# Newton's steps of a second batch on the whole array, and an uneven last tile, in a planned attention and FFN kernel

## The chip, the cores and the metric

The kernel runs on one core of a Trainium2 chip. Times are device microseconds of one execution. Before the change the median of three runs is 261.45 us (261.41 to 261.6). The profile is of one further execution, which took 260.83 us.

The core's engines are PE (matrix products, with its weight loads shown as PEld), DVE and ACT (elementwise work), POOL (which here issues most loads, and does a little elementwise work) and SP (which issues the stores). Each runs its own instructions in order and waits on semaphores for the others.

## The reference

For each of 8 batches and 8 heads, with 576 tokens of 64 dimensions, attention is approximated through 32 landmarks, each the mean of 18 consecutive tokens. Three small softmax matrices are formed; the middle one is inverted by six Newton steps. The result goes through a feed-forward layer with a squared relu (4608 tokens, 512 to 2048 to 512).

```python
A = sm(q, k_lm)
Bm = sm(q_lm, k_lm)
C = sm(q_lm, k)
Z = Bm.transpose(0, 1, 3, 2) / (norm1(Bm) * norminf(Bm) + 1e-06)
for _ in range(6):
    Z = 2 * Z - Z @ Bm @ Z
x = A @ Z @ C @ v
h = x @ w_in
g = np.maximum(h, 0.0) ** 2
return g @ w_out
```

## The kernel before

All work is cut into named steps. A step is declared by `op(name, engines, emit, R, W, ...)`: the engines that may do it with an assumed duration for each, what it reads and writes, and the PSUM banks it needs. `Plan.schedule` (line 134) then runs a list schedule at build time: among the ready steps of an engine the one with the largest `tail` goes first, and where two engines may do a step, the one that ends it first by the plan gets it. `tail` is the length of the work that follows a step, plus an entry for the kind and batch in the table `URGE` (line 1302); `LEAN` (line 1318) shifts the choice between ACT and DVE. The result fixes which engine does each step and in what order. On the chip nothing is reordered: an engine that comes to a step whose input isn't there waits, and everything behind it waits too.

The steps of a batch b that the text names:

- `ld…`, `win`, `wout`, `la`: loads, issued by POOL in the planned order. They are spread over eight semaphores, so a load is issued only when the eighth before it has landed. X holds q and k, V holds v, AC landmark sums that DMA forms for batches 4 to 7.
- `T` (line 576, DVE): transposes of q and k, four a batch. `lm` (lines 593 and 600, PE) sums tokens to landmarks; `lmc`, `lme`, `lmt` bring them to SBUF (ACT, DVE).
- `SC`, `SA`, or `SS` where both are merged (lines 720 and 709, PE): the products for C and A. `B` (line 691): that for Bm.
- `Bmx`, `Bsb`, `Bex`, `Bsu`, `Brc`, `Bml`, `Btf`, `Btr`, `Bcs`, `Bct`, `Bnm`, `Bad`, `Brn`, `Zi`, `Yi` (lines 765 to 852, mostly DVE, `Bex` and sometimes `Btr` on ACT): softmax of Bm, its norms, and Newton's starting values. `BBT` is Bm times its transpose.
- `N` and `U` (lines 874 or 879, and 888): one Newton step is a product on PE and an update on DVE. For batches in `TILED` the eight heads are eight separate 32x32 products per step (line 879). For the others (`whole`) the heads are put on the diagonals of two 128x128 matrices BD by `bd` (line 827; `bt` does so for `BBT`), on POOL or DVE, and two whole-array products do the step (line 874).
- `Cmx`, `Cng`, `Cex`, `Crc`, `Cnr`, `CT`: softmax of C and its transpose. `CV` (line 939): C times v. `Zm`, `ZC` (line 978): Newton's result times that; `ZCe` copies it. `W` (line 1002) multiplies it with w_in, `We` copies the result to WP (a copy of 128x1024).
- `At`, `Amx`, `Asb`, `Aex`, `Asu`, `Arc`, `Aml`, `Ab` (lines 1043 to 1063; `Aex` on ACT, the rest on DVE): softmax of A in two parts, transposed to AT.
- `F` (line 1105, PE): blocks of the first FFN product, from WP and AT. Batches 0 and 1 have 32 blocks (16 of 320 columns, then 16 of 256), the others 16 of 576. `R` (line 1123 on ACT, 1125 on DVE) is the relu, `Q` (line 1132 on ACT, 1134 on DVE) the square into G. PSUM for F is limited to four banks, and RS, between R and Q, has three buffers.
- `O` (line 1152, PE): the second FFN product, 36 tiles of 128 tokens, each in four steps of four 512-column products. `Oe` copies a tile out of PSUM, `St` stores it. The last tile, 35, is done in two parts of 256 columns (steps O35.0 to O35.7), each with its own copy and stores, so that the last store is small. The stores of the first part are both issued by SP, those of the second by SP and ACT.

Until the first O step, fill products (line 1258) keep PE busy in its gaps; they compute nothing that is used.

Of the kernel before, what the change touches and what calls it, by code (L numbers as in the profile page):

```python
# [8 lines left out]
P = 128  # L9
AF = mybir.ActivationFunctionType  # L10
ALU = mybir.AluOpType
AX = mybir.AxisListType
# [8 lines left out]
M = 32  # L21
SEG = S // M
HALF = S // 2
D_MODEL = 512
# [3 lines left out]
N_TILE = N_TOK // P  # L28
# [3 lines left out]
A_LEN = (10, 8)  # L32
# [304 lines left out]
def v_(n, fast=False):  # L337
    return 0.07 + (0.00052 if fast else 0.00104) * n
# [21 lines left out]
def pos_a(c, r):  # L360
    return (c + r + 2) % 4
# [18 lines left out]
def kernel(  # L380
# [106 lines left out]
    def eng(e):  # L487
        return {"ACT": nc.scalar, "DVE": nc.vector, "POOL": nc.gpsimd}[e]
# [46 lines left out]
    def attention(b):  # L535
# [197 lines left out]
        def sCA(e, i):  # L733
            u = i ^ int(pSs[0].at > pSs[1].at)
            for w in range(2):
                for r in range(2):
                    for c in range(4):
                        mmC(c, r, w, u, pSs[i].at + r)
                        mmA(c, r, w, i)
# [8 lines left out]
        if merged:  # L748

            for i in range(2):  # L750
                with_b = i == 0 and b in B_SS
                op(f"SS{b}.{i}", {"PE": 0.42 if with_b else 0.32},
                   lambda e, i=i, with_b=with_b: [sCA(e, i), with_b and sB(e, pSs[0], HALF)],
                   R=[*kA(0), *kA(1)], W=[pSs[i], pAs[i]], alloc=[pSs[i], pAs[i]], mode="32x32",
                   ni=96 if with_b else 64)
        late = [x for t in range(2) for r in range(2) for x in kts(t, r)] if b in B_LATE else []
        if b in B_SS:
            pB, oB = pSs[0], HALF
        else:
            op(f"B{b}", {"PE": 0.14}, lambda e: sB(e, pB, 0), R=[kLT(0), kLT(1), *late], W=[pB],  # L760
               alloc=[pB], mode="64x32" if by_pe else "32x32", ni=16 if by_pe else 32)
# [148 lines left out]
        for r in range(2):  # L910
            R = [*pSs] if merged else [pSs[r]]
            op(f"Cng{b}.{r}", {"DVE": 0.07}, lambda e, r=r: nc.vector.tensor_scalar(  # L912
                out=s_[:, 12 + r:13 + r], in0=s_[:, 12 + r:13 + r], scalar1=-SCALE / SEG,
                scalar2=None, op0=ALU.mult), R=[kb(f"cmx{r}")], W=[kb(f"cmx{r}")])
            op(f"Cex{b}.{r}", {"ACT": a_(576) + 0.27}, lambda e, r=r: nc.scalar.activation(  # L915
                Cs[r][:].rearrange("p x u -> p u x"), cbanks(r),
                AF.Exp, bias=s_[:, 12 + r:13 + r], scale=SCALE / SEG,
                accum_out=s_[:, 14 + r:15 + r]),
               R=[*R, kb(f"cmx{r}")], W=[("C", r), kb(f"csm{r}")], after=[*o_mx[1:], *([o_bsb] if b in B_SS else [])] if merged else ())
            op(f"Crc{b}.{r}", {"DVE": 0.1}, lambda e, r=r: nc.vector.reciprocal(  # L920
                s_[:, 14 + r:15 + r], s_[:, 14 + r:15 + r]), R=[kb(f"csm{r}")], W=[kb(f"csm{r}")])
            op(f"Cnr{b}.{r}", {"DVE": 0.29, "ACT": 0.66}, lambda e, r=r: copy(
                e, Cs[r][:].rearrange("p x u -> p (x u)"), Cs[r][:].rearrange("p x u -> p (x u)"),
                scale=s_[:, 14 + r:15 + r]), R=[("C", r), kb(f"csm{r}")], W=[("C", r)], port=("DVE",))
            op(f"CT{b}.{r}", {"DVE": 0.02 + v_(288)}, lambda e, r=r: nc.vector.transpose(
                CT[:, :, r].rearrange("p s m e -> p s (m e)").bitcast(U32),
                Cs[r][:].rearrange("p (s m) u -> p s (m u)", s=9).bitcast(U32)),
               R=[("C", r)], W=[("CT", r)])
# [87 lines left out]
        def sA(e, us):  # L1016
            for u in us:
                for w in range(2):
                    for c in range(4):
                        for r in range(2):  # L1020
                            mmA(c, r, w, u)
        for us in () if merged else ((0,), (1,)) if b in SPLIT_A else ((0, 1),):

            op(f"SA{b}.{us[0]}",
               {"PE": sum(pe(M * A_LEN[u], 1 if by_pe else 2) for u in us) + 0.02},
               lambda e, us=us: sA(e, us), after=[o_bcs, o_bbt] if b in SA_LATE else (),
               R=kA(0), W=[pAs[u] for u in us], alloc=[pAs[u] for u in us],
               mode="64x32" if by_pe else "32x32", ni=(16 if by_pe else 32) * len(us))
        for u in range(2):
# [3 lines left out]
            ksa = ("SA", u)  # L1033
            fl = lambda a: a[:].rearrange("p r s m -> p (r s) m")
            pairs = lambda a: a[:].rearrange("p r (s e) m -> p (r s) e m", e=2)
            bA = lambda i, sx=sx, n=n: sx[:, i].rearrange("p r s -> p (r s)").unsqueeze(2) \
                .to_broadcast([P, 2 * n, M])
            bE = lambda i, sx=sx, n=n: sx[:, i].rearrange("p r (s e) -> p (r s) e", e=2) \
                .unsqueeze(3).to_broadcast([P, n, 2, M])

            def aT(e, sa=sa, pS=pS, n=n):
                for z in range(2):
                    nc.vector.transpose(sa[:, z].rearrange("p s m -> p (s m)"),  # L1043
                                        ps[:, pS.at + z, 0:M * n])
            op(f"At{b}.{u}", {"DVE": 2 * v_(M * n)}, aT, R=[pS], W=[ksa])
            op(f"Amx{b}.{u}", {"DVE": v_(nn)}, lambda e, sa=sa, sx=sx: nc.vector.tensor_reduce(
                sx[:, 0].rearrange("p r s -> p (r s)"), fl(sa), axis=AX.X, op=ALU.max),
               R=[ksa], W=[("amx", u)])
            op(f"Asb{b}.{u}", {"DVE": v_(nn), **({"POOL": g_(nn)} if b in POOL_A else {})},
               lambda e, sa=sa, bA=bA: eng(e).tensor_tensor(fl(sa), fl(sa), bA(0), ALU.subtract),  # L1050
               R=[ksa, ("amx", u)], W=[ksa], port=("POOL", "DVE"))
            op(f"Aex{b}.{u}", {"ACT": a_(nn)}, lambda e, sa=sa: nc.scalar.activation(  # L1052
                fl(sa), fl(sa), AF.Exp, scale=SCALE / SEG), R=[ksa], W=[ksa])
            op(f"Asu{b}.{u}", {"DVE": v_(nn)}, lambda e, sa=sa, sx=sx: nc.vector.tensor_reduce(
# [85 lines left out]
    def ffn2(ti):  # L1140
# [1 line left out]
        i = ti % N_OS  # L1142
        f2_ops[ti] = []

        parts = ((0, 256), (256, 512)) if ti == N_TILE - 1 else ((0, D_MODEL),)
        for h, (c0, c1) in enumerate(parts):
            po = Bank(1, "o")
            w = c1 - c0
# [11 lines left out]
            def st(e, js, c0=c0, c1=c1):  # L1160
                for j in js:
                    b, s = divmod(2 * ti + j, 9)
                    rows = out[b * S:(b + 1) * S, c0:c1].rearrange(
                        "(m s e) c -> s m e c", s=9, e=2)[s]
                    (nc.scalar if e == "ACT" else nc.sync).dma_start(
                        rows, OS[i][64 * j:64 * j + 64, c0:c1])
# [1 line left out]
               lambda e, c0=c0, c1=c1, po=po: copy(e, OS[i][:, c0:c1], bank(po)[:, 0:c1 - c0]),  # L1168
               R=[po], W=[("OS", i, h)] + ([("OS", i, 1)] if len(parts) == 1 else []))
            R = [("OS", i, h)] + ([("OS", i, 1)] if len(parts) == 1 else [])  # L1170
            if h == 0:
                op(f"St{ti}", {"SP": 1.2}, lambda e, st=st: st(e, (0, 1)), R=R, W=[],
                   nbytes=512 * w, queue="hw")
            else:
                op(f"St{ti}.1", {"SP": 0.6}, lambda e, st=st: st(e, (0,)), R=R, W=[],
                   nbytes=256 * w, queue="hw")
                op(f"St{ti}.2", {"ACT": 0.6}, lambda e, st=st: st(e, (1,)), R=R, W=[],
                   nbytes=256 * w, queue="hw")


# [81 lines left out]
    with tc.manual_schedule():  # L1262
        for o in sorted(pl.ops, key=lambda o: (o.start, o.seq)):
# [3 lines left out]
PLAN_OUT = None  # L1267
FIRST_LOADS = [("kq", 0), ("v", 0), ("k", 1), ("q", 1), ("win", 0), ("win", 1), ("v", 1), ("wout", 0),
               ("wout", 1), ("wout", 2), ("wout", 3)]
TILED = (0, 1)  # L1270
CRIT = {"lm", "lmc", "lme", "lmt", "lte", "B", "Bmx", "Bsb", "Bex", "Bsu", "Brc", "Bml", "Bmb", "Btf", "Bct", "Btr", "Bcs",
        "Bnm", "Bad", "Brn", "BBT", "Zi", "Yi", "N", "U", "ZC", "ZCe", "W", "We", "AZ", "Az"}
CRIT_B = (0,)
# [7 lines left out]
LM_RANK = (4,)  # L1281

AZ = ()

B_SS = ()

# [13 lines left out]
STRETCH = (1.2, 2.5)  # L1300

URGE = {
# [13 lines left out]
}  # L1316

LEAN = {
# [4 lines left out]
}  # L1323
POOL_A = ()
POOL_M = ()
# [40 lines left out]
```

## Time and profile before

| what | value |
| --- | --- |
| median of three runs | 261.45 us |
| profiled execution | 260.83 us, span 259.1 us |
| granted TensorE clock | 1.00 |
| PE busy | 241.3 us (93%) |
| DVE busy | 209.3 us (81%) |
| ACT busy | 177.7 us (69%) |
| POOL busy | 77.6 us (30%) |
| second FFN product (line 1152) on PE | 133.2 us busy in 553 recorded products |
| first FFN product (line 1105) on PE | 76.9 us busy in 512 products |
| fill products (line 1258) | 10.7 us busy |
| loads by POOL (software queue) | 29.89 MB, 63.9% of 16 engines' span |

A busy PE in such a table is not a PE at its peak, since products overlap and their ends are modelled. What a step costs PE is read from the start of its first weight load to that of the next step. So taken, four 512-column products of line 1152 take 0.86 us, and eight 288-column ones of line 1105 0.98 us.

### The profile page before, as it was taken

What the parts mean: (1) busy time and instruction counts of PE and PEld (TensorE: products, weight loads), DVE (VectorE), ACT (ScalarE), POOL (GpSimd) and SP (SyncE); (2) the same over time, 40 slices, a digit from 0 to 9 for tenths busy, and PEclk for the clock granted to TensorE, in tenths of its full rate; (3) what the DMA queues carried; (4) which work ended last, traced back from release to release, by engine and by line L of the source; (5) the groups of instructions that cost most, each with busy time, mean ns of one, the idle gap of its engine ahead of it and who ended that gap; (6) DMA issues with size and microseconds to landing.
All of it is one profiled execution on the core that took longest, in us unless ns stands there. A gap on an engine that the chain in (4) does not pass through costs nothing.

```text
span 259.1 us, 7447 instructions
## 1 busy us (share of the span) xinstructions
PE 241.3 (93%) x2945; PEld 133.3 (51%) x2987; DVE 209.3 (81%) x614; ACT 177.7 (69%) x362; POOL 77.6 (30%) x111
## 2 busy tenths in 40 slices
PE   5779899998998999999999999999999999999993
PEld 1535355445545456565553456466445654466552
DVE  2599999998979999999999999966896689564200
ACT  2123899586989688885746799899586775597410
POOL 8444532346463437343346054210010000000000
PEclk9999999999999999999999999999999999999999
DMA  5999999999999999999989999482104102111043
GB/s 99 203 195 206 207 206 210 228 253 263 224 208 240 228 284 225 198 180 260 188 138 151 303 154 188 77 152 50 44 22 102 44 23 62 43 40 43 20 102 81
DMA packets 25730, 39.80 MB, mean 154 GB/s; under 512 B 4832, under 2 KB 13408, under 8 KB 25696
## 3 DMA queue, kind: packets, MB, share of 16 engines
q0 software_dynamic: 19776, 29.89, 63.9%
q1 hardware_dynamic: 5840, 9.38, 13.2%
q8 instruction: 23, 0.38, 0.5%
q14 instruction: 11, 0.09, 0.1%
q10 hardware_dynamic: 80, 0.07, 0.1%
HBM read 46.14 MB, written 9.44 MB: 214 GB/s over the span
## 4 chain that ended last, share of the span: by engine, by line
PE 59%; DMA 23%; DVE 9%; ACT 4%; issue 3%; POOL 1%; SPq 0%; ACTq 0%; POOLq 0%
PE ps L1152 35%; PE ps L1105 17%; DMA X<-in_q_dram 10%; DMA V<-in_v_dram 7%; DMA w_in<-in_moe_w_in_dram 4%; PE ps L1002 2%; DMA out_dram<-OS 2%; ACT RS L1123 2%; PE ps L939 1%; PE ps L720 1%; DVE G L1134 1%; POOL X L506 1%; DVE TT L576 1%; ACT OS L493 1%; PE ps L874 1%
## 5 line engine op out<-in xcount | busy, mean ns | idle before, releaser
L1152 PE MATMUL ps<-w_out,G 128*128 128x512 bf16 (+1 forms) x553 | 133.2, 373 | 4.0 <-issue 1.9
L1123 ACT ACTIVATE RS<-ps 128x576 bf16<-128x576 f32 (+2 forms) x153 | 77.5, 560 | 12.6 <-PE ps L1105 10.3
L1152 PEld LDWEIGHTS <-G 128*128 128x128 bf16 x592 | 53.7, 98 | 53.4 <-issue 6.5
L1105 PE MATMUL ps<-AT,WP 128*128 128x288 bf16 (+2 forms) x512 | 76.9, 286 | 1.8 <-ACT RS L1123 0.6
L1105 PEld LDWEIGHTS <-WP 128*128 128x128 bf16 x512 | 48.0, 97 | 26.9 <-issue 4.3
L1134 DVE TENSOR_TENSOR G<-RS 128x576 bf16<-128x576 bf16 (+2 forms) x111 | 44.0, 406 | 7.6 <-ACT RS L1123 6.4
L493 ACT COPY OS<-ps 128x512 f32<-128x512 f32 (+1 forms) x34 | 19.6, 578 | 25.9 <-PE ps L1152 22.8
L576 DVE STREAM_TRANSPOSE TT<-X 128x576 uint32<-128x576 uint32 x32 | 24.0, 764 | 6.7 <-DMA X<-in_k_dram 5.2
L493 ACT CAST WP<-ps 128x1024 bf16<-128x1024 f32 x24 | 23.4, 1018 | 4.0 <-PE ps L1002 3.9
L1132 ACT ACTIVATE G<-RS 128x256 bf16<-128x256 bf16 (+2 forms) x49 | 24.1, 523 | 0.6
L888 DVE SCALAR_TENSOR_TENSOR ST<-ST,ps 128x128 bf16<-128x128 bf16 (+1 forms) x48 | 12.8, 266 | 9.7 <-PE ps L874 8.9
L634 POOL DMA_DIRECT2D AC<-in_k_dram x12 | 12.7, 1056 | 21.2 <-DMA AC<-in_k_dram 14.2
L1052 ACT ACTIVATE SA<-SA 128x640 f32<-128x640 f32 (+1 forms) x16 | 11.0, 687 | 9.6 <-DVE SA L1050 9.5
L515 POOL DMA_DIRECT2D V<-in_v_dram x24 | 13.3, 602 | 13.7 <-DMA w_out<-in_moe_w_out_dram 5.8
L639 POOL DMA_DIRECT2D AC<-AC x8 | 10.4, 1301 | 21.4 <-DMA AC<-in_q_dram 12.0
L634 POOL DMA_DIRECT2D AC<-in_q_dram x12 | 14.5, 1208 | 5.1 <-DMA AC<-in_q_dram 3.9
L915 ACT ACTIVATE C<-ps,sm 128x576 bf16<-128x576 f32 x16 | 13.9, 900 | 2.3 <-DVE sm L912 2.2
L1043 DVE STREAM_TRANSPOSE SA<-ps 128x320 f32<-128x320 f32 (+1 forms) x32 | 13.4, 456 | 0.8 <-PE ps L709 0.8
L506 POOL DMA_DIRECT2D X<-in_k_dram x16 | 9.2, 575 | 13.7 <-DVE TT L576 2.9
L497 DVE CAST WP<-ps 128x1024 bf16<-128x1024 f32 x8 | 9.7, 1210 | 3.7 <-PE ps L1002 3.0
L1060 DVE TENSOR_TENSOR An<-SA,smA 128x640 bf16<-128x640 f32 (+1 forms) x16 | 12.5, 790 | 0.1
L1258 PE MATMUL ps<-onesb 128*128 128x512 bf16 x32 | 10.7, 459 | 2.0 <-DVE onesb L462 1.5
(93 smaller groups left out, 263.6 us busy)
## 6 DMA issues: line engine op xcount, KB each, us to landing
out_dram<-OS SPq DMA_DIRECT2D x70, 128.0 KB, 3.9
X<-in_k_dram POOLq DMA_DIRECT2D x16, 288.0 KB, 10.3
X<-in_q_dram POOLq DMA_DIRECT2D x16, 288.0 KB, 10.7
AC<-in_k_dram POOLq DMA_DIRECT2D x12, 384.0 KB, 9.0
AC<-in_q_dram POOLq DMA_DIRECT2D x12, 384.0 KB, 10.3
V<-in_v_dram POOLq DMA_DIRECT2D x8, 288.0 KB, 10.3
w_in<-in_moe_w_in_dram POOLq DMA_DIRECT2D x8, 256.0 KB, 10.4
w_out<-in_moe_w_out_dram POOLq DMA_DIRECT2D x4, 512.0 KB, 12.0
```

The lines of the kernel that those rows point to most:

```text
L493: nc.scalar.copy(o, i)
L515: lambda e, r=r, p0=p0, n=n, src=src: nc.gpsimd.dma_start(vv[32 * p0:32 * (p0 + n), r].rearrange("p s d -> p (s d)"), src),
L576: op(f"T{b}.{t}{r}", {"DVE": v_(576)}, lambda e, r=r: nc.vector.transpose(tt[:, t, r].rearrange("p s m e -> p (s m e)").bitcast(U32), x[:, ...
L634: lambda e, h=h, t=t, src=src: nc.gpsimd.dma_start(flat(ac[:, 2 * t:2 * t + 2]), src[:, :, 6 * D * h:6 * D * h + 6 * D], **(dict(accum_op= ...
L888: nc.vector.scalar_tensor_tensor(out=o, in0=i0, scalar=2.0, in1=bank(pN)[:, 0:2 * w].rearrange("p (r w) -> p r w", r=2), op0=ALU.mult, op1 ...
L915: op(f"Cex{b}.{r}", {"ACT": a_(576) + 0.27}, lambda e, r=r: nc.scalar.activation(Cs[r][:].rearrange("p x u -> p u x"), cbanks(r), AF.Exp, ...
L1043: nc.vector.transpose(sa[:, z].rearrange("p s m -> p (s m)"), ps[:, pS.at + z, 0:M * n])
L1105: nc.tensor.matmul(ps[:, ph.at + i, 0:w], lhsT=wp[:, r, 128 * f:128 * f + 128], rhs=at[:, r, w * i:w * i + w], start=(r == 0), stop=(r == 1))
L1123: nc.scalar.activation(o, x, AF.Relu)
L1132: nc.scalar.activation(o, x, AF.Square)
L1134: nc.vector.tensor_tensor(o, x, x, ALU.mult)
L1152: nc.tensor.matmul(bank(po)[:, 0:c1 - c0], lhsT=G[:, f, lo:lo + P], rhs=w_out[:, f, c0:c1], start=(f == 0), stop=(f == NF - 1))
```

## The change

Three things change. `TILED` goes from (0, 1) to (0,), so batch 1's Newton steps use block diagonals on the whole array as those of batches 2 to 7 do. The last tile is cut at column 384 instead of 256, and the stores of both of its parts are issued by SP and ACT. And `URGE` and `LEAN` are replaced by other tables, so that the plan comes out with another order and another sharing between the engines.

```diff
@@ ffn2
-        parts = ((0, 256), (256, 512)) if ti == N_TILE - 1 else ((0, D_MODEL),)
+        parts = ((0, LAST_CUT), (LAST_CUT, 512)) if ti == N_TILE - 1 else ((0, D_MODEL),)
...
-            if h == 0:
+            if len(parts) == 1:
                 op(f"St{ti}", {"SP": 1.2}, lambda e, st=st: st(e, (0, 1)), R=R, W=[],
                    nbytes=512 * w, queue="hw")
             else:
-                op(f"St{ti}.1", {"SP": 0.6}, lambda e, st=st: st(e, (0,)), R=R, W=[],
+                op(f"St{ti}.{2 * h}", {"SP": 0.6}, lambda e, st=st: st(e, (0,)), R=R, W=[],
                    nbytes=256 * w, queue="hw")
-                op(f"St{ti}.2", {"ACT": 0.6}, lambda e, st=st: st(e, (1,)), R=R, W=[],
+                op(f"St{ti}.{2 * h + 1}", {"ACT": 0.6}, lambda e, st=st: st(e, (1,)), R=R, W=[],
                    nbytes=256 * w, queue="hw")
@@ tables
-TILED = (0, 1)
+TILED = (0,)
...
+A_ROWS = ()
+A_STEP = 2
+
+LAST_CUT = 384
...
 URGE = {
-    "Ab1": -3.3, "Ab5": 32.5, "Aex2": -0.5, "Aex3": 2.2, "Aml3": -10.4, "Aml4": 2.6, "Aml5": 2.2,
...
+    "Ab0": -1.2, "Ab1": 8.8, "Aex2": -27.4, "Aex4": -5.4, "Aml0": 50.9, "Amx7": 5.5,
...
 LEAN = {
-    "CVe4": -1.87, "CVe7": 0.33, "Cnr1": 0.06, "Cnr6": 0.37, "Oe0": 0.09, "Oe1": -0.12,
...
+    "CVe3": 0.2, "CVe6": -0.23, "Cnr1": 0.11, "Cnr2": -3.21, "Cnr5": -6.27, "Oe1": 0.07,
...
```

The diff also adds a second way to form A's products (`sAr`, used for batches in `A_ROWS`) and moves an offset used only for batches in `B_SS`. Both tuples are empty, so no instruction comes from them. `Amx` and `Asb` address their operands through four dimensions instead of two merged ones; the instructions keep their shapes.

Pieces of the orders that come out, old above new, PE first:

```
lm0.0 lm0.1 SC0.0 B0 SC0.1 BBT0 Bcs0 SA0.0 SA0.1 N0.0 N0.1 N0.2 lm1.0 N0.3 CV0 N0.4 N0.5 B1 ZC0 W0.0 W0.1 F0.0
lm0.0 SC0.0 lm0.1 SC0.1 B0 BBT0 Bcs0 SA0.0 SA0.1 N0.0 N0.1 lm1.0 N0.2 CV0 N0.3 N0.4 N0.5 ZC0 W0.0 W0.1 B1 F0.0

O3.0 O3.1 O3.2 lm3.0 SS2.0 O3.3 F1.0 B2 F1.1 F1.2 F1.3 F1.4 F1.5 F1.6 B3 F1.7 F1.8 O4.0 F1.9 F1.10 O5.0 BBT2 O4.1 F1.11 N2.0 F1.12 F1.13
O3.1 B2 O3.2 lm3.0 SS2.0 F1.0 O3.3 F1.1 F1.2 F1.3 F1.4 F1.5 F1.6 F1.7 BBT2 F1.8 B3 F1.9 F1.10 F1.11 F1.12 N2.0 O5.0 F1.13
```

Around F1's start, ACT and then DVE, in the same way:

```
Oe3.0 R1.0 R1.1 R1.2 Q1.0 Q1.1 Bex2 R1.3 R1.4 R1.5 R1.6 Aex2.0 R1.7 R1.8 Bex3 Q1.6 Q1.7 R1.9
R1.0 Q1.0 Btr2 Oe3.0 R1.1 R1.2 R1.3 Q1.1 Q1.2 Q1.3 R1.4 R1.5 Q1.4 R1.6 R1.7 R1.8 Bex3 Q1.7 R1.9

T3.01 At2.0 lme3.0 Amx2.0 Bmx2 Asb2.0 Bsb2 lmt3.0 Q1.2 Bsu2 Bmx3 Brc2 Q1.3 Bml2 Bsb3 Btf2
T3.01 Bmx2 Ab1.0 Bsb2 Asu1.1 Bsu2 Arc1.1 Brc2 Aml1.1 Bml2 Ab1.1 Btf2
```

Block-diagonal products (`bd`, `bt`) by engine: before, 4 on POOL and 38 on DVE; after, 14 on POOL and 35 on DVE. Among those on POOL are now two of batch 1 and all six `bd` of batch 2.

More of the change, by code (lines that the diff above doesn't have):

```diff
@@ L752, in attention @@
                 op(f"SS{b}.{i}", {"PE": 0.42 if with_b else 0.32},
-                   lambda e, i=i, with_b=with_b: [sCA(e, i), with_b and sB(e, pSs[0], HALF)],
+                   lambda e, i=i, with_b=with_b: [sCA(e, i), with_b and sB(e, pAs[0], M * A_LEN[0])],
                    R=[*kA(0), *kA(1)], W=[pSs[i], pAs[i]], alloc=[pSs[i], pAs[i]], mode="32x32",
@@ L757, in attention @@
         if b in B_SS:
-            pB, oB = pSs[0], HALF
+            pB, oB = pAs[0], M * A_LEN[0]
         else:
@@ L918, in attention @@
                 accum_out=s_[:, 14 + r:15 + r]),
-               R=[*R, kb(f"cmx{r}")], W=[("C", r), kb(f"csm{r}")], after=[*o_mx[1:], *([o_bsb] if b in B_SS else [])] if merged else ())
+               R=[*R, kb(f"cmx{r}")], W=[("C", r), kb(f"csm{r}")], after=o_mx[1:] if merged else ())
             op(f"Crc{b}.{r}", {"DVE": 0.1}, lambda e, r=r: nc.vector.reciprocal(
@@ L1021, in sA, with sAr @@
                             mmA(c, r, w, u)
-        for us in () if merged else ((0,), (1,)) if b in SPLIT_A else ((0, 1),):
+        rows = b in A_ROWS
+        def sAr(e, u, s0, s1):
+            for s in range(s0, s1):
+                for w in range(2):
+                    for c in range(4):
+                        for r in range(2):
+                            nc.tensor.matmul(
+                                ps[quad(pos_a(c, r)), pAs[u].at + r, M * s:M * s + M],
+                                lhsT=tt[quad(c), 0, r, A_LEN[0] * u + s, :, w],
+                                rhs=lt[quad(c), 1, r, :, w], start=(w == 0), stop=(w == 1))
+        for u in range(2) if rows else ():
+            for s0 in range(0, A_LEN[u], A_STEP):
+                op(f"SA{b}.{u}{s0 // A_STEP}", {"PE": 0.22 * A_STEP + 0.02},
+                   lambda e, u=u, s0=s0: sAr(e, u, s0, s0 + A_STEP),
+                   after=[o_bcs, o_bbt] if b in SA_LATE else (), R=kA(0), W=[pAs[u]],
+                   alloc=[] if s0 else [pAs[u]], mode="32x32", ni=32 * A_STEP)
+        for us in () if merged or rows else ((0,), (1,)) if b in SPLIT_A else ((0, 1),):
             op(f"SA{b}.{us[0]}",
@@ L1035, in attention @@
             pairs = lambda a: a[:].rearrange("p r (s e) m -> p (r s) e m", e=2)
-            bA = lambda i, sx=sx, n=n: sx[:, i].rearrange("p r s -> p (r s)").unsqueeze(2) \
-                .to_broadcast([P, 2 * n, M])
             bE = lambda i, sx=sx, n=n: sx[:, i].rearrange("p r (s e) -> p (r s) e", e=2) \
@@ L1044, in aT @@
                                         ps[:, pS.at + z, 0:M * n])
[L1045 to L1048, printed above, removed]
+            if rows:
+                raw = lambda pS=pS, n=n: pair(pS, M * n).rearrange("p r (s m) -> p r s m", m=M)
+                kraw = pS
+            else:
+                raw, kraw = lambda sa=sa: sa[:], ksa
+                op(f"At{b}.{u}", {"DVE": 2 * v_(M * n)}, aT, R=[pS], W=[ksa])
+            op(f"Amx{b}.{u}", {"DVE": v_(nn)}, lambda e, raw=raw, sx=sx: nc.vector.tensor_reduce(
+                sx[:, 0], raw(), axis=AX.X, op=ALU.max), R=[kraw], W=[("amx", u)])
             op(f"Asb{b}.{u}", {"DVE": v_(nn), **({"POOL": g_(nn)} if b in POOL_A else {})},
-               lambda e, sa=sa, bA=bA: eng(e).tensor_tensor(fl(sa), fl(sa), bA(0), ALU.subtract),
-               R=[ksa, ("amx", u)], W=[ksa], port=("POOL", "DVE"))
+               lambda e, sa=sa, sx=sx, raw=raw, n=n: eng(e).tensor_tensor(
+                   sa[:], raw(), sx[:, 0].unsqueeze(3).to_broadcast([P, 2, n, M]), ALU.subtract),
+               R=[kraw, ("amx", u)], W=[ksa], port=("POOL", "DVE"))
             op(f"Aex{b}.{u}", {"ACT": a_(nn)}, lambda e, sa=sa: nc.scalar.activation(
```

33 rows, old and new, of tables (LEAN, URGE) are left out of this document.

## The prediction

> **What bounds the kernel now.** I read the page first (busy shares, the slices, the chain that ended last), then busy time by stretch, then the chain and the timelines of single engines. Steps are named as in the code: N1.3 is Newton's product 3 of batch 1, U its update, F1.5 the sixth block of the first FFN matrix for batch 1, R and Q its relu and square, O7.2 a quarter of output tile 7, lm the landmark sums. Each engine runs in order, so rows can be counted off against the written order of both programs.
>
> ```profile
> PE 241.3 (93%) x2945; PEld 133.3 (51%) x2987; DVE 209.3 (81%) x614; ACT 177.7 (69%) x362; POOL 77.6 (30%) x111
> ...
> PE   5779899998998999999999999999999999999993
> ...
> DVE  2599999998979999999999999966896689564200
> ...
> PE 59%; DMA 23%; DVE 9%; ACT 4%; issue 3%; POOL 1%; SPq 0%; ACTq 0%; POOLq 0%
> ```
>
> PE is busy nearly throughout, and DVE is as full until slice 26 (about 168 us). The chain is DMA first, then PE.
>
> ```profile
> 52.00:61.00 9.00, 7.94 (x140) 4.33 (x136) 7.67 (x16) 6.22 (x10) 4.32 (x7) 1.00 1.09 265
> 61.00:69.00 8.00, 7.59 (x78) 4.27 (x77) 7.90 (x35) 7.49 (x22) 4.95 (x8) 1.00 1.11 239
> 69.00:85.00 16.00, 14.84 (x153) 7.93 (x153) 13.96 (x52) 13.91 (x41) 6.94 (x10) 1.00 1.13 221
> ...
> 121.00:142.00 21.00, 20.78 (x224) 10.74 (x227) 20.85 (x62) 11.56 (x23) 9.52 (x11) 1.00 0.91 176
> ```
>
> Columns: length, busy PE, PEld, DVE, ACT, POOL, granted clock, DMA share, GB/s. PE idles 1.06 us in 52 to 61 and 1.16 us in 69 to 85, but only 0.22 us in 121 to 142: behind 110 us there is almost nothing left to gain.
>
> ```profile
> 47.75 11.00 DMA X<-in_q_dram
> 58.75 0.14 issue
> 58.89 1.18 PE ps L600 x36
> ```
>
> This is the last place where a load sets the pace: lm3.0 waits for the q of batch 3. O3.2, the step ahead, starts at 57.04, so 1.81 us pass where four 512-column products take 0.86: a wait of 0.95 us.
>
> **The sum.** The profiled execution took 260.83 us (span 259.1, 1.73 around it), 0.62 below the median of 261.45. I add differences to the profiled time and move the result up by 0.62. The diff names two edits, but it also replaces the tables that set the order of all steps, so the order is where the time can go.
>
> (a) Newton of batch 1. Per product eight 32-row matmuls become two (56 pairs of weight load and matmul against 14), and 7 block-diagonal products are added: five on DVE at 0.20 (rows of L827, start to next start), two on POOL at 0.69. On PE, N steps of either kind take 0.15 to 0.17 us: nothing. The DVE's 1.0 us lies in a stage where DVE is full, but its work from Bmx0 to Bmx2, added up row by row, is 44.4 us in the new order and 46.8 in the old, because other steps move to ACT and POOL. In itself the edit costs 0, with the outcome in (b).
>
> (b) The start, up to lm3.0.
>
> ```profile
> 18.55 0.24 PE L879 MATMUL ps<-ST 32*32 32x64 bf16 x8 [0.22 <-DVE ST L888]
> 19.18 0.24 PE L879 MATMUL ps<-ST 32*32 32x64 bf16 x8 [0.40 <-DVE ST L888]
> 19.35 2.14 PE L593 MATMUL ps<-X,ident 128*128 128x256 bf16 x18
> 21.42 0.24 PE L879 MATMUL ps<-ST 32*32 32x64 bf16 x8
> ...
> 28.07 0.72 PE L1105 MATMUL ps<-AT,WP 128*128 128x320 bf16 x4 [0.38 <-ACT WP L493]
> ```
>
> The 2.1 us of lm1.0 stand ahead of N0.3 now, and ahead of N0.2 in the new order; they can't start sooner, since they wait for a load. So four Newton steps instead of three follow them, at 0.63 each (18.55 to 19.18). Aml0.0 and Arc0.0 (0.96 us of DVE) now stand between U0.5 and the last Zm, and Amx0.1 and Asb0.1 (1.2 us) among the updates; as the updates leave DVE part of that time anyway, I add 0.3: F0.0 comes about 0.9 us late. What of it reaches lm3.0? PE's wait of 0.95 there would swallow it whole (0). Against that, U1.5 has 41.7 us of DVE rows ahead of it instead of 38.6, which moves ZC1 and W1 from 51.2 to about 55, close to lm3.0; then all 0.9 arrives. I take +0.6, ends 0 and +0.9.
>
> (c) F1.0 to F1.13.
>
> ```profile
> 61.99 1.10 ACT L1123 ACTIVATE RS<-ps 128x320 bf16<-128x320 f32 x3
> 62.97 0.83 ACT L1132 ACTIVATE G<-RS 128x320 bf16<-128x320 bf16 x2
> 63.69 0.26 ACT L769 ACTIVATE Bl<-Bl 128x64 f32<-128x64 f32 x1
> 63.84 1.42 ACT L1123 ACTIVATE RS<-ps 128x320 bf16<-128x320 f32 x4
> ```
>
> A relu costs ACT 0.35 us, a square there 0.38, and F may run four blocks ahead of R. Before, O4.0, O4.1 and O5.0 stand among F1.0 to F1.12: PE has 13 x 0.27 + 3 x 0.86 + 0.5 for the small steps = 6.6 us and takes 7.54 (61.09 to 68.63), 0.9 lost. In the new order F1.1 to F1.12 have no O between them; O3.3 and O5.0 stand at the two ends. ACT's row up to R1.9 holds ten relus, six squares, Btr2 (0.24), Oe3.0 (0.55) and Bex3 (0.26): 3.5 + 2.3 + 1.05 = 6.8 us. PE has 3.5 + 1.7 + 0.4 = 5.6. Also, Btr2 stands second in ACT's row and needs Btf2, which is queued on DVE behind the last transpose of batch 3 and 2.9 us of other rows: up to 1 us more. All relus of F1 are queued behind it, and F1.5 waits for them. So 1.2 to 2.3 us are lost in place of 0.9: +0.3 to +1.4. I take +1.1, near the upper end, because the transpose that Btf2 stands behind waits for the same load as lm3.0.
>
> (d) F1.13 to about 110 us. Before, 41.2 us pass from F1.13 (68.63) to F3.0 (109.83) for 38.6 us of PE work, counted with F at 0.21 and 0.49, O at 0.86, N and BBT at 0.15, SS at 0.45, CV at 0.76, ZC at 0.27, W at 0.29: 2.6 us lost. The O4 tile, kept back, can fill such holes; six block-diagonal products of batch 2 (1.2 us) and two evictions of WP (1.13 each) leave DVE. Ends: 0 and -2.6; between 69 and 85 PE's idle time proper is 1.16, and of that I take most, -0.9.
>
> (e) The last tile.
>
> ```profile
> 253.26 0.37 ACT L493 COPY OS<-ps 128x256 f32<-128x256 f32 x1 [1.16 <-PE ps L1152]
> 255.07 0.42 DVE L497 COPY OS<-ps 128x256 f32<-128x256 f32 x1 [12.72 <-DMA out_dram<-OS]
> 255.52 0.64 ACTq L1165 DMA_DIRECT2D out_dram<-OS  x1
> ```
>
> The PE work stays 16 x 512 columns if 128-column products aren't held up by weight loads: ZC's four pairs with 64 columns start every 29 ns (L978), so 54 ns is safe. The last copy shrinks from 256 to 128 columns: 0.42 to about 0.29 (a 512-column one takes about 0.69). The stores land in 2.0 to 2.4 us whether they carry 64 or 128 KB, so smaller ones gain little. ACT now issues one store of the first part: 0.37 to 0.5 for its copy and 0.64 for the issue fit into the 0.87 us of the second part plus its copy. I take -0.15, ends -0.35 and +0.2.
>
> The Trainium skill, TensorE: Matmul & The Clock Gate, Back-to-back issue gap, gives about 81 ns for each pair of weight load and 128-column product. By it the second part would take 16 x 81 = 1.30 instead of 0.87 us, and the sum would be 0.4 higher; the 29 ns in the trace speak against it.
>
> Sum: 0 + 0.6 + 1.1 - 0.9 - 0.15 = +0.65. 260.83 + 0.65 + 0.62 = 262.1.
>
> **Rivals.** *Faster.* DVE decides more than PE's order: its work up to Bmx4 is 103.6 us against 104.4, and it waits 1.6 us for PE and ACT between 73 and 77 before, which the new order fills. Then (d) gives -2.1, (b) is swallowed by the wait for the load (0), and (c) ends at +0.6: with (e) -1.65, 259.8. For it speaks that DVE is full; against it, that F1 hangs on ACT. It decides if Btf2 ends before ACT is through with Q1.0.
>
> *No change.* (b) 0 for the wait at lm3.0, (c) +1.1 and (d) -1.1, since every hole filled later is only one made earlier: 261.3.
>
> *POOL's row.* POOL gets 14 block-diagonal products instead of 4, at 0.69 each, among the load issues. The six of batch 2 lengthen each Newton step by 0.5. In the new order N2.5 stands behind O8.2, ten us later than now, which leaves room; if each comes late at its place in PE's row, PE waits up to 6 x 0.5 = 3 us, and X for batches 5 and 6 behind them too. I price it at 2 beyond the forecast: 264.1.
>
> The Trainium skill, SBUF, Who interferes with whom, says that DVE and GpSimd exclude each other for a whole instruction where both read two SBUF operands. The trace does not show it: a square of 0.32 us starts at 66.97 while such a product runs on POOL until 67.02. If six of the 14 met a square for half their length, 6 x 0.35 = 2.1 us would come on top.
>
> **Chances.** Forecast 0.42, faster rival 0.33, no change 0.17, POOL 0.08. A measurement of this kernel tells about 0.2% (0.52 us) from nothing. Of the forecast's share I count 0.06 as within that bound and 0.02 as faster: faster 0.35, same 0.23, slower 0.42. The forecast's own range is 261.5 to 263.1; with the rivals and the ends of (b) to (e), 259.4 to 263.5: outside lie a third of the faster rival and most of POOL's.
>
> **What would show it.** F0.0 at about 29.0; lm3.0 at 59.3 to 59.8, with no wait for a load ahead of it; PE idle before F1.5 to F1.13 with ACT full, and Btr2 waiting for DVE; PE's lost time between F1.13 and F3.0 under 2 us; the last DVE copy near 0.3 us. Wrong would be an lm3.0 still at 58.9 behind a wait, or F1.13 before 68.5, or PE waiting for POOL at N2.x.

## The result, and the profile after

The changed kernel takes 264.28 us (median of 4 runs, 263.82 to 264.75), the kernel before on the same chip 261.43: a ratio of 1.0109, 95% interval 1.009 to 1.0128. A second sample in a later group of runs gave 1.0132 (1.0096 to 1.0167). The change costs about 3 us. The profiled execution took 263.82 us, with a span of 262.1 (before: 259.1).

The page of the changed kernel, busy time and the chain that ended last:

```profile
PE 245.6 (94%) x2948; PEld 133.0 (51%) x2948; DVE 209.3 (80%) x602; ACT 183.3 (70%) x371; POOL 84.9 (32%) x121
...
PE 44%; DVE 25%; DMA 18%; ACT 5%; issue 3%; POOL 2%; SPq 0%; POOLq 0%; DVEq 0%; ACTq 0%
```

DVE's share of the chain went from 9% to 25%, and PE's from 59% to 44%: there is a stretch now in which DVE sets the pace. (How much it costs, these shares don't tell: in the faster e1 below, DVE has 35%.) Busy time by stretch (columns as in the prediction) shows where:

```profile
52.00:61.00 9.00, 8.78 (x146) 3.77 (x145) 8.50 (x21) 5.73 (x10) 3.64 (x7) 1.00 1.10 245
61.00:69.00 8.00, 5.97 (x53) 3.25 (x52) 7.79 (x28) 7.65 (x23) 5.66 (x8) 1.00 1.09 261
69.00:85.00 16.00, 14.58 (x165) 7.84 (x178) 15.03 (x46) 13.52 (x38) 9.76 (x14) 1.00 1.13 215
...
121.00:142.00 21.00, 20.89 (x230) 11.71 (x228) 19.66 (x61) 16.38 (x33) 10.65 (x12) 1.00 1.00 185
```

The wait for a load ahead of lm3.0 is gone (PE 8.78 of 9.00 in 52 to 61, before 7.94). From 61 to 69 PE idles 2.03 us instead of 0.41, while DVE stays full. At its end begin batch 2's Newton steps (N2.0 at 68.30, N2.3 at 80.63), whose block diagonals POOL now makes; from 69 to 85 PE idles another 1.42 us. The waits between 60 and 85 us (engine, line, releaser: sum, times, longest) name it:

```profile
PEld L874 <- POOL BD L827: 1.9, 2, 1.0
...
PE ps L874 <- POOL BD L827: 1.1, 2, 0.6
...
ACT RS L1144 <- DVE G L1155: 1.0, 1, 1.0
```

PE waits for POOL at N2.0 and N2.1 (L874). How the product comes late is seen in POOL's own row (start, length, line, operation, in brackets the idle time before it and its releaser):

```profile
67.00 0.55 POOL L506 DMA_DIRECT2D X<-in_k_dram  x1 [0.40 <-PE ps L1126]
67.56 0.68 POOL L827 TENSOR_TENSOR BD<-ST,blkb 128x256 bf16<-128x256 bf16 x1
68.59 0.58 POOL L506 DMA_DIRECT2D X<-in_k_dram  x1 [0.34 <-DMA X<-in_q_dram]
70.30 0.54 POOL L506 DMA_DIRECT2D X<-in_q_dram  x1 [1.12 <-DMA X<-in_q_dram]
70.85 0.68 POOL L827 TENSOR_TENSOR BD<-ST,blkb 128x256 bf16<-128x256 bf16 x1
```

The input of bd2.0 (Yi2, L852) was written at 66.41, that of bd2.1 (U2.0, L888) at 68.95. The products start 1.15 and 1.90 us later, right behind load issues that were themselves waiting, two of them for earlier transfers. And these products do something to DVE. DVE's row of the changed kernel:

```profile
66.80 1.64 DVE L1155 TENSOR_TENSOR G<-RS 128x320 bf16<-128x320 bf16 x2
...
70.69 1.03 DVE L1155 TENSOR_TENSOR G<-RS 128x320 bf16<-128x320 bf16 x1
...
76.04 1.79 DVE L1155 TENSOR_TENSOR G<-RS 128x256 bf16<-128x256 bf16 x3 [0.28 <-ACT RS L1144]
```

A square takes 0.28 to 0.32 us. The one at 67.25 (the second of the pair at 66.80) takes 1.19, the one at 70.69 1.03, the last of the three at 76.04 1.39; each ends 0.1 to 0.2 us behind a product on POOL. The chain of waits of the changed kernel runs through such a square:

```profile
66.44 0.79 ACT RS L1144 x2
67.23 0.02 issue
67.25 1.19 DVE G L1155
68.44 0.14 DVE sm L771
```

So there were several suspects at the same place: products that come late behind load issues and DVE instructions that can't run beside them, and, as rivals, the new order of PE's steps around F1 and batch 1's Newton on the whole array.

### The profile page after: what moved, and what is told of

Read it like the earlier page. It is cut to its first block, busy times and chain, and to the rows that moved or that the text cites. A ratio compares the mean times of both kernels' runs of the same rounds, so it can differ in the third digit from the quotient of the medians.

```text
span 262.1 us, 7402 instructions
## 1 busy us (share of the span) xinstructions
PE 245.6 (94%) x2948; PEld 133.0 (51%) x2948; DVE 209.3 (80%) x602; ACT 183.3 (70%) x371; POOL 84.9 (32%) x121
## 4 chain that ended last, share of the span: by engine, by line
PE 44%; DVE 25%; DMA 18%; ACT 5%; issue 3%; POOL 2%; SPq 0%; POOLq 0%; DVEq 0%; ACTq 0%
PE ps L1173 27%; PE ps L1126 13%; DMA w_out<-in_moe_w_out_dram 5%; DVE G L1155 4%; DMA X<-in_q_dram 4%; DMA X<-in_k_dram 4%; DMA w_in<-in_moe_w_in_dram 4%; ACT RS L1144 3%; DVE TT L576 2%; PE ps L1002 2%; DVE smA L1075 2%; DVE sm L907 2%; DVE SA L1059 2%; DVE smA L1067 2%; POOL X L506 1%
## 5 line engine op out<-in xcount | busy, mean ns | idle before, releaser
L1173 PE MATMUL ps<-w_out,G 128*128 128x512 bf16 (+2 forms) x592 | 140.2, 374 | 0.2
L1144 ACT ACTIVATE RS<-ps 128x576 bf16<-128x576 f32 (+2 forms) x158 | 80.2, 558 | 19.1 <-PE ps L1126 15.7
L1155 DVE TENSOR_TENSOR G<-RS 128x576 bf16<-128x576 bf16 (+2 forms) x104 | 42.4, 420 | 9.9 <-ACT RS L1144 9.0
L1153 ACT ACTIVATE G<-RS 128x576 bf16<-128x576 bf16 (+2 forms) x56 | 32.0, 594 | 0.6
L493 ACT COPY OS<-ps 128x512 f32<-128x512 f32 (+1 forms) x30 | 17.5, 582 | 19.7 <-PE ps L1173 18.9
L493 ACT CAST WP<-ps 128x1024 bf16<-128x1024 f32 x22 | 21.4, 1019 | 2.9 <-PE ps L1002 2.9
L827 POOL TENSOR_TENSOR BD<-ST,blkb 128x256 bf16<-128x256 bf16 x13 | 9.6, 736 | 28.5 <-DVE ST L888 23.6
L497 DVE CAST WP<-ps 128x1024 bf16<-128x1024 f32 x10 | 12.1, 1218 | 7.0 <-PE ps L1002 5.3
L888 DVE SCALAR_TENSOR_TENSOR ST<-ST,ps 128x128 bf16<-128x128 bf16 (+1 forms) x48 | 12.6, 262 | 5.2 <-PE ps L874 5.2
L634 POOL DMA_DIRECT2D AC<-in_q_dram x12 | 15.3, 1279 | 1.6 <-DMA X<-in_k_dram 0.9
L634 POOL DMA_DIRECT2D AC<-in_k_dram x12 | 13.6, 1132 | 6.5 <-DVE LM L642 3.2
L497 DVE COPY OS<-ps 128x512 f32<-128x512 f32 (+1 forms) x7 | 4.4, 625 | 13.6 <-DMA out_dram<-OS 13.6
```

What stands on the lines that cost most here:

```text
L493: nc.scalar.copy(o, i)
L497: eng(e).tensor_copy(o, i)
L634: lambda e, h=h, t=t, src=src: nc.gpsimd.dma_start(flat(ac[:, 2 * t:2 * t + 2]), src[:, :, 6 * D * h:6 * D * h + 6 * D], **(dict(accum_op= ...
L1144: nc.scalar.activation(o, x, AF.Relu)
L1153: nc.scalar.activation(o, x, AF.Square)
L1155: nc.vector.tensor_tensor(o, x, x, ALU.mult)
```

## The experiments

Theory T1 blames POOL's products, T2 the order of the steps around F1, T3 batch 1's Newton on the whole array. All runs keep the order that the planner wrote and alter one thing as the operations are emitted. Beside the medians I use one stretch of the profile, from the start of lm3.0 to the end of PE's last weight load ("PE's end"), because the start of F0.0 varied between 27.9 and 30.7 us over the profiled executions. With the new last tile this weight load lies 0.11 us nearer to the end of the last product, so only before and e3, which have the old one, read 0.11 lower beside the others. "DVE longer" is the time that the same DVE instructions between 64 and 95 us take beyond those of e1, block diagonals left out.

| run | median us | ratio to before (95%) | lm3.0 to PE's end | DVE longer |
|---|---|---|---|---|
| before | 261.43 | 1 | 195.83 | |
| changed | 264.28 | 1.0109 (1.009 to 1.0128) | 198.71 | 3.27 |
| e9, changed again | 264.46 | 1.0132 (1.0096 to 1.0167) | 199.02 | 2.43 |
| e1, bd2 on DVE | 262.69 | 1.0034 (1.0005 to 1.0062) | 196.40 | 0 |
| e2, no product on POOL | 263.17 | 1.0077 (1.0043 to 1.0112) | 196.81 | |
| e3, before with bd2 on POOL | 264.58 | 1.0112 (1.0076 to 1.0149) | 199.50 | |
| e5, product that nobody reads | 264.75 | 1.0132 (1.0108 to 1.0156) | 199.19 | 2.75 |
| e10, zeros in its place | 262.72 | 1.0066 (1.0044 to 1.0089) | 196.42 | -0.13 |
| e6, loads behind bd2 | 262.27 | 1.0034 (1.0022 to 1.0047) | 196.78 | 1.35 |
| e7, batch 1 in tiles | 262.25 | 1.0037 (1.0017 to 1.0056) | 196.26 | 0.15 |
| e8, BBT2 later | 262.75 | 1.0058 (1.0036 to 1.008) | 196.38 | -0.19 |
| e4, before with the new last tile | 261.03 | 0.998 (0.9958 to 1.0003) | 196.04 | |
| e12, the same again | 261.11 | 1.0003 (0.9987 to 1.002) | 195.82 | |
| e11, as e12, no product on POOL | 260.80 | 1.0001 (0.9978 to 1.0025) | 196.05 | |

The kernel before was run beside each group: medians of 261.41 (e1 to e4), 261.14 (e5 to e8) and 260.89 us (e9 to e12).

**e1: batch 2's six products on DVE.**

```diff
+ON_DVE = tuple(f"bd2.{i}" for i in range(6))
-            o.emit(o.eng)
+            o.emit("DVE" if o.name in ON_DVE else o.eng)
```

> The changed kernel with its order of work as it stands; only the six block diagonals of batch 2's Newton steps (bd2.0 to bd2.5) are computed by DVE, at the place that POOL had them, instead of by POOL. T1 (POOL's products cost the time: PE waits for them at N2.0 and N2.1, together 3.0 us in the waits from 60 to 85 us, and they stretch DVE's squares): 261.5 to 262.8, 1.5 to 2.8 below the changed kernel. T2 (twelve blocks of FFN1 of batch 1 in a row and the postponed tile O4 cost it): 264.0 to 264.8, since that order stays. T3 (batch 1's Newton in full-array products costs it): as T2.

The median is 1.6 us lower, and the stretch behind lm3.0 2.3 shorter. N2.0 starts 8.14 us after lm3.0 instead of 9.00, N2.1 10.66 instead of 12.29, N2.3 19.05 instead of 21.33. Of the 3.45 us that PE idled from 61 to 85, 1.71 are left in the same stretch, 62 to 86 here, most of them in its first 8 us. T1 holds for most of the loss; what is left over before, 0.9 us (0.1 to 1.6), is not POOL's.

**e2: the other eight products on DVE too.** The list of e1 is longer by bd1.2, bd1.5, bd3.1, bd4.3, bd5.3, bd6.2, bd6.5 and bt7.

> As the run before, and the other eight products that POOL has in the changed kernel (bd1.2, bd1.5, bd3.1, bd4.3, bd5.3, bd6.2, bd6.5, bt7) by DVE too. T1: within 0.5 of the run before, mostly below it, as each of the eight stretches a square of DVE or makes PE wait only a little; a gain over 0.5 here would say that batch 2's six are not special. T2 and T3: 264.0 to 264.8.

No gain, though I had expected a small one: 0.4 longer behind lm3.0 than e1, with intervals that overlap. So a product on POOL does not cost as such; batch 2's six are special by where they lie.

**e3: the reverse, in the kernel before.**

```diff
+ON_POOL = tuple(f"bd2.{i}" for i in range(6))
-            o.emit(o.eng)
+            o.emit("POOL" if o.name in ON_POOL else o.eng)
```

> The kernel before with its order of work as it stands; only the six block diagonals of batch 2 go from DVE to POOL. T1: 263.0 to 264.5, 1.5 to 3 above the kernel before, with DVE's squares under a product of POOL at 1.0 to 1.4 us instead of 0.3. T2 and T3: 261.2 to 262.0, since neither the order nor batch 1 is touched.

3.2 us slower, with the old order and the old batch 1. Rows of POOL and PE in this run:

```profile
69.47 0.54 POOL L506 DMA_DIRECT2D X<-in_k_dram  x1 [0.66 <-DMA X<-in_q_dram]
70.03 0.68 POOL L827 TENSOR_TENSOR BD<-ST,blkb 128x256 bf16<-128x256 bf16 x1
```

```profile
70.77 0.23 PE L874 MATMUL ps<-ST,BD 128*128 128x64 bf16 x2 [2.19 <-POOL BD L827]
```

Here it is the queue: bd2.0's input is there at 67.82, two load issues stand ahead of the product, the second waits for a transfer, and PE idles 2.19 us. The product's own 0.68 us is the smaller part. Not all of the loss is the queue's: the input itself is 0.6 us late after lm3.0, because Bad2, which leads to it, took 0.77 us instead of 0.16 beside bt2, a product that POOL has in the kernel before too.

**e6: the changed kernel with its load issues behind the products.** The six products stay on POOL.

```diff
+BEHIND = {"bd2.0": ("ldk5.0",), "bd2.1": ("ldk5.1", "ldq5.0"), "bd2.2": ("ldq5.1", "ldk6.0"),
+          "bd2.3": ("la4.21", "ldk6.1"), "bd2.4": ("la4.20", "ldq6.0"), "bd2.5": ("ldq6.1", "la5.01")}
...
+        for o in sorted(todo, key=lambda o: late.get(o.name, (at[o.name], 0))):
```

> The changed kernel with batch 2's six products on POOL; only POOL's own row is another: the DMA issues that stand between them (loads of batches 5 and 6) come behind the product that they stood in front of. If the products are late because POOL holds issues that wait for earlier transfers ahead of them (bd2.0 began 1.1 us and bd2.1 1.9 us after its input was written): lm3.0 to the end of PE 196.8 to 197.6 instead of 198.7, time 262.8 to 263.6. If only the length of the product counts (0.68 us on POOL, 0.28 on DVE) or the stretched squares: 198.2 to 198.8, time 263.8 to 264.6. Loads that come too late would show as PE waits behind lm5 and make it slower than 264.5.

In its times as fast as e1, behind lm3.0 0.4 longer, and better than I had expected: no wait of PE for POOL is left, and DVE is stretched by 1.35 us instead of 3.27. So six products on POOL, each longer than on DVE, cost little once they come in time. POOL's row now waits for its input instead of for the loads:

```profile
68.12 0.66 POOL L827 TENSOR_TENSOR BD<-ST,blkb 128x256 bf16<-128x256 bf16 x1 [1.01 <-DVE ST L852]
68.73 0.59 POOL L506 DMA_DIRECT2D X<-in_k_dram  x1
69.81 0.75 POOL L827 TENSOR_TENSOR BD<-ST,blkb 128x256 bf16<-128x256 bf16 x1 [0.48 <-DVE ST L888]
```

The loads come later by this, at no cost: from N2.3 to PE's end it takes 177.4 us in e6 and in e1.

**e5: the exclusion by itself.** DVE makes the block diagonals as in e1, and POOL makes each once more at its place in the changed kernel, into a buffer that nobody reads. PE and DVE wait for nothing on POOL.

```diff
-                   W=[("BD", it % 2)], port=("POOL", "DVE"))
+                   W=[("BD", it % 2)], port=("POOL", "DVE")).also = \
+                    lambda a=a: bdiag("POOL", BDX[:], a[:, :, 0, :])
...
             o.emit("DVE" if o.name in ON_DVE else o.eng)
+            if o.name in ON_DVE:
+                o.also()
```

> The run with batch 2's block diagonals on DVE (262.69; from lm3.0 to the end of PE 196.4 us, in the changed kernel 198.7), and POOL forms the same six products once more, at the places that the changed kernel gives them, into a buffer that nobody reads: so nobody waits for POOL, but its products lie beside DVE's squares and its load issues lie behind them as there. If the stretched squares (1.0 to 1.4 us instead of 0.3) are what costs: lm3.0 to the end 197.5 to 198.7, time 263.8 to 264.8. If PE's waiting for the product is what costs: 196.3 to 196.9, time 262.4 to 263.2.

The product that nobody needs costs as much as the whole of e1's gain; behind lm3.0 it is even more than I had expected. No wait of PE or DVE for POOL shows between 60 and 95 us. DVE's row in this run:

```profile
70.72 1.60 DVE L1083 TENSOR_TENSOR An<-SA,smA 128x640 bf16<-128x640 f32 x1
...
73.53 1.10 DVE L820 TENSOR_SCALAR sm<-sm 128x2 f32<-128x2 f32 x1
...
76.28 1.58 DVE L1157 TENSOR_TENSOR G<-RS 128x256 bf16<-128x256 bf16 x3 [0.28 <-ACT RS L1146]
```

and POOL's:

```profile
70.88 0.68 POOL L828 TENSOR_TENSOR BDX<-ST,blkb 128x256 bf16<-128x256 bf16 x1
...
73.91 0.68 POOL L828 TENSOR_TENSOR BDX<-ST,blkb 128x256 bf16<-128x256 bf16 x1
...
76.16 1.14 POOL L828 TENSOR_TENSOR BDX<-ST,blkb 128x256 bf16<-128x256 bf16 x1
```

The same three DVE rows in e1, without a product beside them:

```profile
71.85 0.87 DVE L1081 TENSOR_TENSOR An<-SA,smA 128x640 bf16<-128x640 f32 x1
...
73.93 0.17 DVE L819 TENSOR_SCALAR sm<-sm 128x2 f32<-128x2 f32 x1
...
75.78 0.84 DVE L1155 TENSOR_TENSOR G<-RS 128x256 bf16<-128x256 bf16 x3 [0.27 <-ACT RS L1144]
```

Together they take 2.4 us more in e5. From N2.1 to N2.3 PE takes 10.86 us instead of 8.39: 2.47 more. DVE was full there, and what its row grows by, PE loses one for one.

**e10: is it the reading, or that POOL is busy?** In place of the unread product POOL fills 512 columns with zeros, which takes 0.55 us and reads nothing.

```diff
-                    lambda a=a: bdiag("POOL", BDX[:], a[:, :, 0, :])
+                    lambda: nc.gpsimd.memset(BDX[:], 0.0)
```

> The run with the product that nobody reads (264.75), but in its place POOL fills 128x512 elements with zeros: the same six places in POOL's row, an instruction that reads nothing, and DVE forms batch 2's block diagonals as there. If DVE's two-input squares wait for a POOL instruction that reads SBUF: the squares stay at 0.28 to 0.35 us, N2.1 to N2.3 takes 8.2 to 9.0 us instead of 10.9, time 262.4 to 263.3. If it is only that POOL's load issues come later: N2.1 to N2.3 still over 10 us, time 264 to 265. DVE's one-input casts and scalings may still be stretched if what excludes them is the writing.

Two DVE rows of this run, the first the same as e5's first, and the fills beside them:

```profile
71.77 0.88 DVE L1083 TENSOR_TENSOR An<-SA,smA 128x640 bf16<-128x640 f32 x1
...
74.46 0.76 DVE L1157 TENSOR_TENSOR G<-RS 128x256 bf16<-128x256 bf16 x3
```

```profile
71.99 0.54 POOL L870 MEMSET BDX<- 128x512 bf16 x1
...
74.45 0.54 POOL L870 MEMSET BDX<- 128x512 bf16 x1
```

The fill at 71.99 lies inside the row at 71.77, which keeps its 0.88 us, and the one at 74.45 under three squares that take 0.76 us together, as in e1. No DVE row between 64 and 95 us is longer than there, and N2.1 to N2.3 takes 8.40 us, as in e1. So it is neither POOL being busy nor its late load issues: DVE's products wait for POOL's product, which reads SBUF, and not for its fill, which only writes. No cast and no operation with a constant (such as the 1.10 us row of e5) met a fill, so for these the run says nothing.

The Trainium skill, SBUF — State Buffer, Who interferes with whom, says this: DVE and GpSimd share a pair of ports, held for a whole instruction, and a DVE product with both operands in SBUF contends only with a GpSimd instruction that reads SBUF. e5 and e10 agree on both halves (1.60 against 0.88 us for the same row). It also names DVE's casts and operations with a constant (`tensor_scalar`), where they run in a two-port mode: in e5 the addition of a constant to two columns took 1.10 us instead of 0.17, in the changed kernel a cast 0.59 instead of 0.15; in which mode they ran no run shows. It excepts reductions: one at 131.44 us in e1 keeps its 0.67 us beside a product.

**e7: batch 1's Newton in 32x32 tiles, on top of e1.** The first line changes at both products, BBT and N.

```diff
-                if whole:
+                if whole and b != 1:
...
-            o.emit("DVE" if o.name in ON_DVE else o.eng)
+            if o.name[:3] not in ("bt1", "bd1"):
+                o.emit("DVE" if o.name in ON_DVE else o.eng)
```

> The run with batch 2's block diagonals on DVE, and batch 1's Newton steps in 32x32 tiles as in the kernel before: its seven products (five on DVE, two on POOL) are left out, the order of the rest stays. The prediction's step (a) and T2: F0.0 to lm3.0 within 0.4 of 30.3, time within 0.5 of 262.69. T3 (the full-array products of batch 1 cost it): F0.0 to lm3.0 0.5 to 1.5 shorter, time 261.2 to 262.2.

F0.0 to lm3.0 takes 30.09 us (e1: 30.30), the time agrees with e1's within the intervals. T3 falls: the edit that gave the change its name costs nothing that can be measured.

**e8: BBT2 behind F1.8, on top of e1.**

```diff
+        at["BBT2"] = (*at["F1.8"], 1)
```

> The run with batch 2's block diagonals on DVE, and in PE's row the product BBT2 behind F1.8 instead of in front of it; nothing else moves. In that run BBT2 makes PE wait 0.9 us for its block diagonal at F1.7. T2, in the form that PE's row has BBT2 too early: F1.0 to F1.13 7.0 to 7.2 us instead of 7.43, and 0.2 to 0.4 less at the end. If what follows of batch 2's Newton steps decides instead: F1.0 to F1.13 as before or up to 0.2 longer.

F1.0 to F1.13 takes 7.43 us, as in e1. This form of T2 falls: BBT2 stands where its chain on DVE lets it, and PE's wait only moves.

**e4, e12 and e11: the last tile, and a faster version.** e4 and e12 are the kernel before with the new last tile (its stores issued as in the change, too):

```diff
-        parts = ((0, 256), (256, 512)) if ti == N_TILE - 1 else ((0, D_MODEL),)
+        parts = ((0, 384), (384, 512)) if ti == N_TILE - 1 else ((0, D_MODEL),)
```

> The kernel before with the last tile in parts of 384 and 128 columns and nothing else changed. All theories: 0.15 to 0.35 below the kernel before (261.1 to 261.3). Below 0.1 would say that the end of the changed kernel gained nothing by the cut.

> The kernel before with the last tile in parts of 384 and 128 columns, again, with more rounds, as the version that may beat both kernels: 0.997 to 0.9995 of the kernel before, 260.8 to 261.3.

In the profiles, counted from the start of O35.0, PE's last product ends after 3.87 us with either cut, and the span after 7.76 and 7.77 us instead of 8.03: a gain of 0.26. In the times the two samples give 0.998 and 1.0003: not told from nothing. e11 moves its four products from POOL to DVE:

> The kernel before with the last tile in parts of 384 and 128 columns and its four products of POOL (bt2, bd3.3, bd4.5, bt7) on DVE too. In the profile of before no square lies long under any of the four, and PE waits 0.3 us for bt2 in one run: within 0.4 of the run beside it that has them on POOL, 260.7 to 261.4. Over 0.5 faster would say that every product on POOL costs.

Also no difference. None of these beats the kernel before by more than the measurement.

**e9: the changed kernel again**, beside e10 to e12:

> The changed kernel unchanged, on the chip of the runs beside it: 264.0 to 264.8, 1.009 to 1.013 of the kernel before, by every theory. Nearer to 262.7 would mean that the comparison with the runs on other chips was worth nothing.

It came out as the first time, so comparisons between the groups stand. The granted clock of its profile was 1.00 against 0.99 in the first one, so the clock isn't what costs.

## Why the prediction failed

Direction right, size wrong: +0.65 forecast, +2.9 measured (+3.6 in e9), above the range. The likeliest case was the changed kernel without what POOL's products do; e1 and e7, where that is gone for batch 2, and e6, where most of it is, stand at 1.0034 to 1.0037 of before, +0.9 us, e8 and e10 at 1.0058 and 1.0066. The medians of these five, 262.25 to 262.75, all lie in the forecast's own range (261.5 to 263.1); e2's 263.17 lies just above it.

- **(a)** 0: held (e7).
- **(b)** +0.6, ends 0 and +0.9: lm3.0 came at 59.30 after 58.86, and the wait for the load ahead of it was gone, as forecast. The size can't be read from one pair of executions: lm3.0 varies by 1.5 to 2 us among the profiles of one order. Over the profiles the mean of lm3.0 is 58.8 us in five runs with the old order and 60.1 in nine with the new, so it is rather above the upper end.
- **(c)** +1.1: mis-sized by what POOL added. From lm3.0 to F1.13, with the steps B2, O4.0 and O4.1 taken off that the old order has there (1.9 us), before takes 7.87 us, e1 8.98, the changed kernel 9.72: +1.1 for the order, +1.85 with POOL. That e1 meets the +1.1 is luck in part, for the reason I gave was wrong: PE waited for DVE (0.89 us before BBT2, 0.37 before F1.2), not for ACT, and Btr2 on ACT started without a wait to speak of at 62.38.
- **(d)** -0.9 from F1.13 to F3.0: this is the step that failed. With the prediction's own prices, the new order has 41.3 us of PE work there instead of 38.5 (four O steps more, two W less). Before it takes 41.21 us, 2.75 lost; the changed kernel 44.67, 3.35 lost (+0.6); e1 43.11, 1.79 lost (-0.96). So the -0.9 holds only without the products on POOL. I had credited DVE with the six products that left it (1.2 us) and did not charge it with what they do to it from POOL: 3.27 us.
- Behind F3.0 I assumed no difference; both e1 and the changed kernel lose 0.6 us more there than before, counted in the same way. No run took that apart; it stays open.
- **(e)** -0.15: the profiles give -0.26 for the same cut in e4 and e12, within the ends, though the times can't tell it from 0. The 128-column products of the last part started every 56 ns, near the 54 I had taken and far from the higher figure set beside it. The last copy on DVE took the 0.29 us forecast:

```profile
258.28 0.29 DVE L497 COPY OS<-ps 128x128 f32<-128x128 f32 x1 [13.58 <-DMA out_dram<-OS]
```

The rival *POOL's row* named the place and, with 264.1, nearly the time, and I gave it 0.08. The number is luck in part: it priced the greater length of six products, which e6 shows to cost little; what cost was that they came late and kept DVE out. Two readings made it look unlikely. One was that N2.5 stands ten us later in the new order, "which leaves room": the room is behind N2.3, and the loss came at N2.0 to N2.3. The other was the row with which I set the exclusion aside: a square from 66.97 beside a product that ended at 67.02. An overlap of 0.05 us at the product's very end could not show a square waiting for it. It was no evidence, and the rule of the Trainium skill, whose price I had put at up to 2.1, was what decided.

The kernel's own text held a second sign. The plan keeps POOL's products and DVE's squares apart: both kinds of step are marked with `port` (lines 868 and 1158 of the changed kernel), and a step so marked isn't started while another holds it (line 209, in `Plan.schedule`):

```python
if e in o.port and port > t + 1e-9:
    continue
```

So in the plan no product lies beside a square. In the profile before, POOL's four products stand beside reductions, transposes, a cast and two operations with a constant, and beside a square only for those 0.05 us: it could hardly show the rule. In the changed kernel the products came 1.15 and 1.90 us after their input, and so met squares from which the plan had kept them away.

The sum for the changed kernel then reads, from rows: 0.27 up to lm3.0 (its 0.44, less 0.17 for B2, already done), 1.85, 0.60, 0.60 and -0.37 from PE's last weight load to the end of the span, together 2.95, by which the span grew. Of it e1 gives back 2.3, 0.74 in (c) and 1.56 in (d).

How much is exclusion and how much lateness? e5 shows that exclusion alone suffices (+2.8 behind lm3.0 over e1). In the changed kernel DVE's row grows by 3.27 and is relieved of 1.2: 2.1 net, and PE loses 2.3. In e9 the sums fit less well (2.43 less 1.2, against 2.6): there no square lay under bd2.0, and DVE instead waited 0.86 us for N2.0, which waited for the product. e3 shows lateness costing PE 2.19 us at one step. Both have one root: a product on POOL runs when the load issues ahead of it let it, not when its input is there.

## What to carry to other kernels

Before an element-wise step goes to POOL, look at what stands ahead of it in POOL's row and what that waits for, and at what DVE runs at that time: if DVE is full and reads two operands from SBUF, an overlap can cost DVE the product's whole length and more. When a written rule speaks against a change, and a row seems to refute it, ask first how long the two instructions really overlapped. And cost an operation that is moved off a full engine on both engines, not only on the one that it leaves.

## What was not expected of the hardware

- A DVE instruction that is kept out shows in the trace as a long instruction, not as idle time: the busy share of DVE hides it (19.1 of 20 us between 60 and 80 us in e5, 19.2 in e1, though PE was busy for 2.1 us less in e5). It is found by comparing the length of the same row between kernels.
- The addition of a constant to two columns (0.17 us) can take 1.10 us in this way, so small links of a chain are hit as well as large squares. In e5 it starts at 73.53, before the product's recorded start at 73.91, so the recorded starts on POOL don't mark the exclusion exactly.
- It isn't always DVE that pays. At bd2.4 in the changed kernel, a DVE row with two inputs from SBUF began first and kept the length that it has in e1 (0.69); POOL's product took 1.05 us instead of 0.68, and then the square behind that row 0.66 instead of 0.29. Yet the square at 70.69 also began before its product (70.85) and took 1.03. What decides who goes first was not tried. The rows at bd2.4, DVE and POOL:

```profile
81.52 0.68 DVE L1070 TENSOR_TENSOR SA<-SA,smA 128x512 f32<-128x512 f32 x1
82.22 0.66 DVE L1155 TENSOR_TENSOR G<-RS 128x256 bf16<-128x256 bf16 x1
```

```profile
81.69 1.05 POOL L827 TENSOR_TENSOR BD<-ST,blkb 128x256 bf16<-128x256 bf16 x1 [2.66 <-DVE ST L888]
```

- bd2.3, two places behind the issue of an accumulating load (L634), is recorded as 1.14 to 1.16 us where 0.68 is usual, in the changed kernel, e9 and e5; its record begins before that of the issue ahead of it ends. This need not be exclusion: a fill in e10, which reads nothing, has 1.06 us at that place instead of 0.54.
- Kernels whose work is the same up to there start F0.0 at times that lie 1.6 us apart and more (28.01 us in e11, 29.61 in e12). What decides that was not tried.
